# Ring buffers and w_out moved to multiples of 2 KB in a partition, and one block of output products placed earlier in the tail

## The chip, the core and the metric

The kernel runs on one core of a Trainium2 chip. A core has a TensorE (PE, with its weight loads listed apart as PEld), a VectorE (DVE), a ScalarE (ACT), a GpSimd (POOL) and a SyncE (SP), which here only issues transfers, and sixteen DMA engines that carry them. On-chip memory has 128 partitions; a tile occupies the same bytes in each of them. The metric is the device time of one execution in microseconds (us), less is better.

## What is computed

One decoding step of attention over a cached window, gated by a small MLP. From the reference, cut to what matters:

```python
xn = _layernorm(x)                                   # x: (2, 1, 512)
# attention: 32 query heads, 8 key/value heads of 128, window of the last 4096 positions
q = (xn @ wq) as (2, 32, 1, 128)
p = softmax(q . k[:, :, Sk - W:, :] * 128 ** -0.5)
s = (p . v[:, :, Sk - W:, :]) as (2, 1, 4096) @ wo   # wo: (4096, 512)
# gate
z = _gelu(xn @ w_in)                                 # w_in: (512, 1792)
z1, z2 = z[..., :896], _layernorm(z[..., 896:])
g = _silu((z1 * (w_sp * z2 + b_sp)) @ w_out)         # w_out: (896, 512)
out = x + s * g
```

All arrays are float32. Two batches times eight key/value heads are 16 pairs (batch, head); each needs 2 MB of keys and 2 MB of values, and with wq and wo (8 MB each), w_in and w_out the core reads 89.4 MB once.

## The kernel before

**Memory.** Four pools hold the tiles. "cst" (one buffer for each name) has w_out and the small constants; "ring" has four slots of 32 KB in a partition, tagged "slot"; "sb" has the working tiles, two of each; "ps" the accumulators. Pools lie one behind the other in the order in which they are opened (lines 73 to 76). Before the first pool, 128 bytes of a partition hold constants of the framework, behind an area that it reserves; so "cst" begins at byte 16,512, with w_out as its first tile, and "ring" at 55,680.

**The ring.** w_in takes a slot of it, then wq in two slots, then the 16 pairs, keys in the first half of a slot and values in the second, and at last two slots of wo. All these loads are issued by SyncE in program order (lines 89 to 98, "load" in lines 112 to 118, and lines 496 to 509). A load waits until the work that read its slot before is done: for a pair, that is the second product with the values four pairs earlier. Every load covers all 128 partitions, with one piece of consecutive bytes for each partition: 16 KB for keys or values, 28 KB for w_in, 14 KB for w_out, 32 or 16 KB for wq, and 16, 8, 4 or 2 KB for wo. Such a piece is called a row below.

**The attention loop** (lines 462 to 493) interleaves three pairs by hand: for the current one, DVE transposes the keys in four pieces ("turn"), and TensorE multiplies them with the queries ("shares", "scores"); for the one before, maximum, exponentials, and TensorE's product with the values ("pv"); for the one before that, the collection of its heads. The order on every engine is the program's order.

**The tail** (lines 496 to 568). The heads fall into three sets: heads 0 to 3, 4 and 5, 6 and 7. The first two sets' share of wo is loaded as blocks 0 and 1 (8 parts each, 2 MB) and blocks 2 and 3 (4 parts each, 1 MB); the third set's as blocks 4 to 7 (4, 2, 1 and 1 parts). The transfers go in the order of these numbers. "wo_early(n, a0)" multiplies four parts of block n, from part a0, into the accumulator "part", one part for each of the four groups of 32 rows of it; the counter "done" picks the group, and the first four and the last four calls open and close the sums. The products of blocks 2 and 3 stand in a hand-written order among those of block 0 and 1 (lines 540 to 548). Then ACT copies "part" to "parts" (line 550), blocks 4 to 7 are multiplied into "so" as they land, "parts" is added to it by four more products (lines 560 to 564), and DVE applies the gate and adds x.

Of the kernel before, what the change touches and what calls it, by code (L numbers as in the profile page):

```python
# [9 lines left out]
F32 = mybir.dt.float32  # L10
# [4 lines left out]
P = 128  # L15
# [26 lines left out]
def kernel(  # L42
# [27 lines left out]
    DC = D // G  # L70
    SCALE = DH ** -0.5

    cst = ctx.enter_context(tc.tile_pool(name="cst", bufs=1))
    ring = ctx.enter_context(tc.tile_pool(name="ring", bufs=4))
    sb = ctx.enter_context(tc.tile_pool(name="sb", bufs=2))
    ps = ctx.enter_context(tc.tile_pool(name="ps", bufs=1, space=bass.MemoryType.PSUM))

# [435 lines left out]
    def wo_early(n, a0=0):  # L513
        nonlocal done
        t, oT, j = blocks[n]
        for a in range(a0, a0 + 4):
            g = done % G
            pe.matmul(
                part[32 * g : 32 * g + 32, :], oT[:, j + a, :], t[:, a, :], start=(done < G), stop=(done >= EARLY - G)
            )  # L520
            done += 1
# [22 lines left out]
    wo_early(0, 4)  # L544
    wo_early(2)
    wo_early(1, 0)
    wo_early(3)
    wo_early(1, 4)
    parts = sb.tile([P, D], F32, tag="o", name="parts")
    act.activation(parts, part, AF.Copy)  # L550
    so = bank("so", DC)
# [45 lines left out]
```

## Time and profile before

| | us |
|---|---|
| three runs, median | 219.85 |
| the three runs | 219.77, 221.17, 219.85 |
| the profiled execution, device time | 219.7 |
| its span, first to last instruction | 217.6 |
| TensorE busy | 153.0 |
| VectorE busy | 123.4 |
| ScalarE busy | 49.7 |
| mean granted TensorE clock | 0.85 of full |

The profile is of one execution. The span leaves out 2.1 us of the time around the first and last instruction. "Busy" is the time in which an engine had an instruction in work. A row of the forty slices gives, for each slice of 5.44 us, tenths of that slice in which the engine was busy; for the clock, tenths of full speed that were granted to TensorE. In rows of instructions, "out<-in" names the tiles written and read, "x8" counts instructions, and in brackets stand the idle time of the engine just before and what ended it ("issue" is the engine's own sequencing). A product of float32 operands shows as two instructions.

### The profile page before, as it was taken

What the parts mean: (1) busy time and instruction counts of PE and PEld (TensorE: products, weight loads), DVE (VectorE), ACT (ScalarE), POOL (GpSimd) and SP (SyncE); (2) the same over time, 40 slices, a digit from 0 to 9 for tenths busy, and PEclk for the clock granted to TensorE, in tenths of its full rate; (3) what the DMA queues carried; (4) which work ended last, traced back from release to release, by engine and by line L of the source; (5) the groups of instructions that cost most, each with busy time, mean ns of one, the idle gap of its engine ahead of it and who ended that gap; (6) DMA issues with size and microseconds to landing.
All of it is one profiled execution on the core that took longest, in us unless ns stands there. A gap on an engine that the chain in (4) does not pass through costs nothing.

```text
span 217.6 us, 2755 instructions
## 1 busy us (share of the span) xinstructions
PE 153.0 (70%) x1068; PEld 51.8 (24%) x1068; DVE 123.4 (57%) x249; ACT 49.7 (23%) x128; POOL 5.2 (2%) x19
## 2 busy tenths in 40 slices
PE   0179694653898179886788859567995888479593
PEld 0128421300222022221222212112231212124232
DVE  4511212674775577887889494857667494842001
ACT  4110202201213211433223222331142223232000
POOL 8000000000000000000000000000000000000000
PEclk9999589958569755999999978996589589999669
DMA  7999999999999999999999999999999999999990
GB/s 254 425 431 470 392 425 429 428 428 431 425 428 431 428 425 434 425 422 429 428 428 425 428 425 431 429 431 422 428 428 422 428 428 434 434 428 416 416 376 30
DMA packets 6524, 89.57 MB, mean 412 GB/s; under 512 B 734, under 2 KB 750, under 8 KB 1136
## 3 DMA queue, kind: packets, MB, share of 16 engines
q1 hardware_dynamic: 6492, 89.40, 97.0%
q8 instruction: 8, 0.13, 0.2%
q14 instruction: 4, 0.03, 0.0%
q10 hardware_dynamic: 20, 0.01, 0.0%
HBM read 89.40 MB, written 0.00 MB: 411 GB/s over the span
## 4 chain that ended last, share of the span: by engine, by line
DMA 56%; PE 20%; DVE 18%; ACT 3%; issue 1%; SPq 0%; ACTq 0%
DMA kv<-in_A_k_cache_dram 35%; DVE kts L36 14%; DMA wq<-in_A_wq_dram 11%; DMA wo<-in_A_wo_dram 10%; PE acc L36 6%; PE sh L36 4%; PE s L36 3%; PE part L36 3%; PE q_ps L36 2%; DVE m L36 2%; ACT ss L36 1%; PE so L36 1%; ACT p L36 1%; DVE gate L36 1%; DVE pT L36 1%
## 5 line engine op out<-in xcount | busy, mean ns | idle before, releaser
L36 DVE STREAM_TRANSPOSE kts<-kv 128x1024 f32<-128x1024 f32 x64 | 77.2, 1226 | 20.8 <-DMA kv<-in_A_k_cache_dram 20.8
L36 PE MATMUL sh<-kts,qb 128*32 128x512 f32 x256 | 42.5, 740 | 32.8 <-DVE mg L36 24.3
L36 PE MATMUL acc<-kv,pT 128*16 128x512 f32 x256 | 35.0, 669 | 0.0
L36 ACT ACTIVATE o<-acc,wd 128x128 f32<-128x128 f32 x64 | 18.2, 367 | 58.6 <-PE acc L36 50.6
L36 PE MATMUL s<-ss,sums 128*128 128x512 f32 x32 | 21.8, 768 | 6.2 <-ACT ss L36 6.2
L36 ACT ACTIVATE p<-s,nb 128x512 f32<-128x512 f32 x16 | 11.0, 688 | 45.9 <-DVE nb L36 45.9
L36 DVE STREAM_TRANSPOSE pT<-p 128x512 f32<-128x512 f32 x16 | 11.4, 712 | 14.7 <-ACT p L36 14.7
L36 PEld LDWEIGHTS sh<-kts,qb 128*32 128x32 f32 x256 | 6.7, 121 | 51.8 <-issue 37.1
L36 PEld LDWEIGHTS acc<-kv,pT 128*16 128x16 f32 x256 | 6.8, 115 | 26.9 <-issue 19.3
L36 ACT ACTIVATE ss<-sh 128x512 f32<-128x512 f32 x16 | 9.6, 597 | 15.1 <-PE sh L36 13.8
L36 PE MATMUL q_ps<-wq,xnT 128*32 128x512 f32 x64 | 9.3, 704 | 5.1 <-DMA wq<-in_A_wq_dram 5.0
L36 DVE TENSOR_REDUCE m<-s 128x1 f32<-128x512 f32 x16 | 10.5, 657 | 1.4 <-PE s L36 1.4
L36 PEld LDWEIGHTS mo<-l,heads 128*128 128x128 f32 x32 | 5.6, 219 | 17.2 <-ACT p L36 17.2
L36 PE MATMUL part<-wo,oT 128*32 128x512 f32 x48 | 7.9, 792 | 2.3 <-DMA wo<-in_A_wo_dram 2.3
L36 PEld LDWEIGHTS mo<-mg,joint 128*128 128x128 f32 x32 | 5.6, 219 | 16.2 <-issue 15.4
L36 PE MATMUL col<-o,selw 128*32 128x128 f32 x128 | 7.5, 310 | 1.6 <-ACT o L36 1.4
L36 PE MATMUL z<-win,xnT 128*32 128x448 f32 x32 | 4.9, 776 | 4.2 <-DMA win<-in_B_w_in_dram 4.2
L36 PEld LDWEIGHTS s<-ss,sums 128*128 128x128 f32 x32 | 5.6, 219 | 9.2 <-ACT ss L36 6.7
L36 PE MATMUL mo<-l,heads 128*128 128x1 f32 x32 | 6.9, 285 | 0.4
L36 PE MATMUL mo<-mg,joint 128*128 128x8 f32 x32 | 7.1, 293 | 0.0
L36 PE MATMUL zT_ps<-rowm,z 128*128 128x2 f32 x28 | 6.6, 370 | 0.0
L36 DVE TENSOR_TENSOR res<-so,gate 128x128 f32<-128x128 f32 x1 | 0.3, 291 | 11.1 <-PE so L36 11.1
(107 smaller groups left out, 82.9 us busy)
## 6 DMA issues: line engine op xcount, KB each, us to landing
kv<-in_A_k_cache_dram SPq DMA_DIRECT2D x16, 2048.0 KB, 18.9
kv<-in_A_v_cache_dram SPq DMA_DIRECT2D x16, 2048.0 KB, 22.2
wq<-in_A_wq_dram SPq DMA_DIRECT2D x1, 4096.0 KB, 24.4
wq<-in_A_wq_dram SPq DMA_DIRECT2D x2, 2048.0 KB, 30.0
wo<-in_A_wo_dram SPq DMA_DIRECT2D x2, 2048.0 KB
win<-in_B_w_in_dram SPq DMA_DIRECT2D x1, 3584.0 KB
wo<-in_A_wo_dram SPq DMA_DIRECT2D x3, 1024.0 KB, 25.7
wout<-in_B_w_out_dram SPq DMA_DIRECT2D x1, 1792.0 KB, 15.2
```

The lines of the kernel that those rows point to most:

```text
L36: return self.tc.keep_in_program_order(call(*args, **kwargs))
```

## The change

Two edits. The ring's pool is opened ahead of "cst", behind a new pool with one tile "fit" of 480 floats (1,920 bytes in a partition), which nothing writes or reads. The ring thus begins at 16,512 + 1,920 = 18,432, nine times 2,048; its four slots take 131,072 bytes, and w_out, the first tile of "cst", begins at 149,504, 73 times 2,048. The other tiles of "cst" and all of "sb" move as well. In the tail, "wo_early(1, 4)", the second half of block 1, stands ahead of "wo_early(3)" where it stood behind it.

```diff
     SCALE = DH ** -0.5
 
+    fit = ctx.enter_context(tc.tile_pool(name="fit", bufs=1))
+    fit.tile([P, 480], F32, tag="fit", name="fit")
+    ring = ctx.enter_context(tc.tile_pool(name="ring", bufs=4))
     cst = ctx.enter_context(tc.tile_pool(name="cst", bufs=1))
-    ring = ctx.enter_context(tc.tile_pool(name="ring", bufs=4))
     sb = ctx.enter_context(tc.tile_pool(name="sb", bufs=2))
     ps = ctx.enter_context(tc.tile_pool(name="ps", bufs=1, space=bass.MemoryType.PSUM))
...
     wo_early(0, 4)
     wo_early(2)
     wo_early(1, 0)
+    wo_early(1, 4)
     wo_early(3)
-    wo_early(1, 4)
     parts = sb.tile([P, D], F32, tag="o", name="parts")
     act.activation(parts, part, AF.Copy)
```

## The prediction

> **What bounds the kernel now.** I read the page first: the busy shares, the forty slices, the packets and the chain.
>
> ```profile
> span 217.6 us, 2755 instructions
> PE 153.0 (70%) x1068; PEld 51.8 (24%) x1068; DVE 123.4 (57%) x249; ACT 49.7 (23%) x128; POOL 5.2 (2%) x19
> PEclk9999589958569755999999978996589589999669
> DMA  7999999999999999999999999999999999999990
> GB/s 254 425 431 470 392 425 429 428 428 431 425 428 431 428 425 434 425 422 429 428 428 425 428 425 431 429 431 422 428 428 422 428 428 434 434 428 416 416 376 30
> DMA packets 6524, 89.57 MB, mean 412 GB/s; under 512 B 734, under 2 KB 750, under 8 KB 1136
> q1 hardware_dynamic: 6492, 89.40, 97.0%
> DMA 56%; PE 20%; DVE 18%; ACT 3%; issue 1%; SPq 0%; ACTq 0%
> ```
>
> No compute engine is near full: PE is busy for 70% of the span, DVE for 57%. The transfers are: SyncE's queue takes 97.0% of what sixteen DMA engines could give, and every slice but the first and the last reads 9. The rate is flat: from the sixth slice to the thirty-sixth it lies between 422 and 434 GB/s. 89.40 MB at 428 GB/s is 208.9 us of the 217.6, so what else happens in the middle is covered. The chain says the same with 56% for DMA; its PE and DVE pieces are the times at which a buffer was handed back for a transfer that then stood in the queue anyway. Two rows of the DMA issues show how deep that queue is:
>
> ```profile
> kv<-in_A_k_cache_dram SPq DMA_DIRECT2D x16, 2048.0 KB, 18.9
> kv<-in_A_v_cache_dram SPq DMA_DIRECT2D x16, 2048.0 KB, 22.2
> ```
>
> One of these transfers is 2.10 MB, 4.9 us at 428 GB/s, and takes 18.9 or 22.2 us from issue to landing: about four are queued ahead. A slot given back a few us sooner or later doesn't change when the last byte comes.
>
> Then I asked whether the rate depends on what the engines do, by stretches of 24 to 30 us in the middle:
>
> ```profile
> 36.00:60.00 24.00, 14.50 (x113) 4.56 (x113) 14.44 (x20) 3.44 (x7) 0.00 (x0) 0.72 1.01 427
> 60.00:90.00 30.00, 22.63 (x132) 6.37 (x136) 20.59 (x35) 6.51 (x20) 0.00 (x0) 0.71 1.01 430
> 90.00:120.00 30.00, 23.75 (x176) 6.81 (x168) 25.05 (x44) 9.92 (x28) 0.00 (x0) 1.00 1.01 426
> 120.00:150.00 30.00, 20.71 (x148) 6.45 (x147) 20.88 (x35) 7.54 (x21) 0.00 (x0) 0.92 1.01 427
> 150.00:180.00 30.00, 25.21 (x146) 6.83 (x146) 20.54 (x37) 7.60 (x22) 0.00 (x0) 0.74 1.01 428
> ```
>
> The columns are the stretch, its length, busy us of PE, weight loads, DVE, ACT and POOL, then clock, DMA share and GB/s. PE goes from 14.5 of 24 to 25.2 of 30 us, DVE from 14.4 to 25.1, the clock from 0.71 to 1.00; the rate stays at 426 to 430 with a DMA share of 1.01. Nothing but the DMA engines sets the pace here.
>
> Last the tail, by TensorE's timeline and windows cut where the clock changes:
>
> ```profile
> 202.67 1.26 PE L36 MATMUL part<-wo,oT 128*32 128x512 f32 x8
> 206.20 5.62 PE L36 MATMUL part<-wo,oT 128*32 128x512 f32 x32 [2.27 <-DMA wo<-in_A_wo_dram]
> 211.63 1.06 PE L36 MATMUL so<-wo,oT 128*32 128x128 f32 x32
> 212.59 0.43 PE L36 MATMUL so<-parts,rowm 128*32 128x128 f32 x8
> 212.83 1.21 PE L36 MATMUL so<-wo,oT 128*32 128x128 f32 x32
> ```
>
> ```profile
> 199.90:203.40 3.50, 2.63 (x32) 1.28 (x24) 0.48 (x2) 0.88 (x4) 0.00 (x0) 1.00 0.96 405
> 203.40:206.80 3.40, 1.13 (x8) 0.23 (x8) 0.00 (x0) 0.00 (x0) 0.00 (x0) 0.50 1.00 417
> 206.80:210.20 3.40, 3.40 (x20) 0.90 (x16) 0.00 (x0) 0.00 (x0) 0.00 (x0) 0.50 1.02 416
> 210.20:214.10 3.90, 3.84 (x88) 2.16 (x80) 0.00 (x0) 0.60 (x1) 0.00 (x0) 1.00 0.51 196
> ```
>
> TensorE has nothing to do for 2.27 us until block 2 of wo has landed, works without a gap from 206.20 to 214.04, and does the first 4 us of it at half clock (0.50 until 210.2). So after 206.2 it is TensorE that ends the kernel, closely followed by the last transfers: the DMA share falls to 0.51 from 210.2 on.
>
> **The change part by part.** *The layout.* In the allocated program w_out begins at byte 16,512 of a partition and the ring at 55,680: both 128 past a multiple of 256 (55,680 is 27 × 2,048 + 384). The 1,920 bytes of "fit" put the ring at 18,432 = 9 × 2,048; its four slots are 131,072 bytes, so w_out follows at 149,504 = 73 × 2,048. The working tiles of "sb" move up by 1,920. No instruction, wait or transfer is added, removed or moved: "fit" is never written. So the only term can be the time of one access at its new place.
>
> For engine accesses I take nothing. The cover is the stream: a quicker or slower transpose or matmul of the attention only moves hand-backs that are some four transfers early. That holds until DVE, the chain's second worker, is late: it is busy 25.05 of 30 us in the densest stretch, and so would have to become 30 / 25.05, or 20%, slower before it set the pace.
>
> For the transfers there is one term: rate. The trace has no transfer that starts at another alignment, so I bound it by slices. The best inside the plateau read 434 GB/s, the worst 422. All 89.40 MB at 434 take 206.0 us, 2.9 less than at 428; at 422 they take 211.8, 2.9 more. 6524 packets less 734 under 512 B are 5,790 rows, 362 for each engine, so 2.9 us is 8 ns a row. I take zero: the nearest row is the plateau itself, the same through five stretches, and no row of this trace ties a part of those 8 ns to where a row lands.
>
> [...]
>
> *The order in the tail.* Line 548's four products (second half of block 1) now stand ahead of line 547's (block 3). No count changes: the 32 instructions from 206.20 are eight passes over the four column groups either way, two for each call of wo_early. The weight loads show whether block 3 was ever awaited:
>
> ```profile
> 206.17 0.23 PEld L36 LDWEIGHTS part<-wo,oT 128*32 128x32 f32 x8 [3.34 <-issue]
> 207.02 0.23 PEld L36 LDWEIGHTS part<-wo,oT 128*32 128x32 f32 x4 [0.63 <-issue]
> 207.88 0.23 PEld L36 LDWEIGHTS part<-wo,oT 128*32 128x32 f32 x4 [0.63 <-issue]
> 208.73 0.22 PEld L36 LDWEIGHTS part<-wo,oT 128*32 128x32 f32 x4 [0.63 <-DMA wo<-in_A_wo_dram]
> 209.58 0.23 PEld L36 LDWEIGHTS part<-wo,oT 128*32 128x32 f32 x4 [0.63 <-issue]
> 210.34 0.14 PEld L36 LDWEIGHTS part<-wo,oT 128*32 128x32 f32 x4 [0.53 <-issue]
> 210.77 0.13 PEld L36 LDWEIGHTS part<-wo,oT 128*32 128x32 f32 x4 [0.29 <-issue]
> ...
> 213.61 0.16 PEld L36 LDWEIGHTS so<-wo,oT 128*32 128x32 f32 x8 [0.21 <-DMA wo<-in_A_wo_dram]
> ```
>
> One row goes ahead of each pass. At half clock they stand 0.85 us apart, the one marked with block 3's transfer (208.73) included, so the wait cost nothing; at full clock 0.43 (210.34 to 210.77). Behind the swap it is asked for two passes later, 1.7 us at this clock. Nothing is queued behind it on PE that could have gone before, and ACT's copy of "part" still waits for the eighth pass at 211.8. The price is zero. Were the clock full from 206.2 on, block 3 would be asked for three passes of 0.43 us after 206.17, at 207.5, before it is known to be there, and the old order could stall, the new one hardly; but the end would then wait for the last block (asked for at 213.61, with 0.21 of waiting), and no more than about 0.5 us could be won.
>
> Sum: 0 for the engines, 0 for the rate, 0 for the order. The profiled execution took 219.7 us, its span of 217.6 and 2.1 around it; the median of the three runs is 219.85, 0.15 above. I keep 219.7.
>
> **The rivals.** *The rows get cheaper at the new start.* [...] At the full 2.9 us it is 216.8. For it: a stream at 97.0% where only cost per byte can change. Against it: a plateau so flat looks like a plain ceiling.
>
> *Writes and reads collide at the new places.* Rows of 2 KB read by TensorE and rows written by the DMA engines would then begin at the same offsets, and the stream falls to its worst plateau slice, 422 GB/s: 219.7 + 2.9 = 222.6. Since TensorE already waits for the transfers, every us lost is seen; below 423.5 GB/s it costs over 1%. Against it: the rate didn't react to engine load in any of the five stretches.
>
> *The clock falls otherwise in the tail.* Two more passes at half clock cost 0.84 us, with all that follows at half clock too (the products from 211.63 to 214.04) about 3; full clock from 206.2 wins 0.2 to 0.5. That gives 219.3 to 222.7. [...]
>
> *The change does nothing at all* is my forecast.
>
> **How the numbers follow.** The forecast (219.2 to 220.2) gets 0.52, cheaper rows 0.30 (216.8 to 219.2), collisions 0.08 (220.5 to 222.6), the clock 0.10. About 1%, 2.2 us, is what a measurement of this kernel can tell from no change. Faster by more than that (under 217.65) needs a rate above 432.6 GB/s, or 1.7 us with a kind clock: 0.13 of the 0.30. Slower by more (over 222.05): 0.05 of the collisions and 0.02 of the clock, 0.07. The rest, 0.80, lies within. From 217.6 to 220.9 leaves out 0.12 below and 0.08 above.
>
> **What would show it.** The plateau: 428 GB/s again means the rows cost the same; 431 to 434 means they got cheaper; 422 or less a collision. Block 2's landing, by the start of the 32 products, near 206.2 means no gain from the stream. The weight load marked with block 3's transfer should stand two steps later, at unchanged steps, and the products from block 2 to the end should take 7.8 us if the clock returns four us into them. I am wrong if the plateau moves by 4 GB/s or more, or if the tail changes without the clock or the landing having changed.

## Result, and the profile after

| | before | changed |
|---|---|---|
| median, us | 219.76 (10 runs, 219.65 to 221.17) | 218.33 (10 runs, 218.12 to 219.69) |
| ratio | | 0.9933 (95% interval 0.9912 to 0.9954) |

The kernel became 0.67% faster, 1.43 us: inside the range that was given, and not the "no change" that was its likeliest case. One execution of all those reported below, 225.5 us at a granted clock of 0.65 among the twelve with three pairs off, is left out of that run's ratio. The lines of the changed kernel's page that answer to those shown of before:

```profile
span 217.6 us, 2755 instructions
PEclk9999587665599955999889999699958999558598
DMA  7999899999999999999999999999999999999970
GB/s 254 422 434 482 386 428 429 434 434 428 434 419 431 431 434 431 425 434 429 434 431 434 428 431 428 426 434 434 434 425 434 428 434 425 434 428 425 423 303 2
q1 hardware_dynamic: 6492, 89.40, 96.4%
```

The bytes and packets are the same and the span too, yet the last two slices differ: 303 and 2 GB/s where 376 and 30 stood. The transfers were done sooner and the end didn't follow. This profiled execution, 219.69 us, is the slowest of its ten, so its tail is read apart from its stream. First the stream, in the same five stretches (the last column is GB/s):

```profile
36.00:60.00 24.00, 17.67 (x112) 5.60 (x112) 14.39 (x19) 3.15 (x7) 0.00 (x0) 0.59 1.01 431
60.00:90.00 30.00, 21.67 (x136) 6.24 (x136) 20.79 (x36) 7.40 (x22) 0.00 (x0) 0.83 1.01 430
90.00:120.00 30.00, 24.77 (x176) 7.19 (x172) 25.32 (x44) 9.32 (x27) 0.00 (x0) 0.94 1.01 431
120.00:150.00 30.00, 20.89 (x155) 6.10 (x154) 21.07 (x37) 7.95 (x22) 0.00 (x0) 0.94 1.00 429
150.00:180.00 30.00, 21.89 (x144) 6.21 (x140) 20.50 (x35) 8.34 (x24) 0.00 (x0) 0.89 1.01 431
```

The plateau rose: a mean of 430.4 GB/s, against 427.6 before. For all 89.40 MB that is 207.7 us in place of 209.1, 1.4 less. The packet records of the trace, one for each row, say where it comes from:

```
duration of a row, ns      before                          changed
16 KB (4,608 rows)         611 to 625, mean 615.4          611 for 99.6% of them, mean 612.1
 8 KB   (384 rows)         309 to 327, mean 313.7          309
 4 KB   (128 rows)         159 to 172, mean 164.4          159
 2 KB   (256 rows)         84 (median)                     84
```

A few rows are longer than these ranges and count in the means: 14 of 16 KB before (to 1,273 ns) and 10 after (to 1,158), and two of 4 KB before (378 and 440). The shortest row is the same in both kernels for each of these sizes; what has gone is the scatter above it. For each of the sixteen engines that is 288 × 3.3 + 24 × 4.7 + 8 × 5.4 ns = 1.1 us, most of the 1.4 that the rate gives.

TensorE's tail in this execution:

```profile
200.30 3.62 PE L36 MATMUL acc<-kv,pT 128*16 128x512 f32 x16
203.70 1.93 PE L36 MATMUL part<-wo,oT 128*32 128x512 f32 x8
205.40 0.65 PE L36 MATMUL col<-o,selw 128*32 128x128 f32 x8
206.47 1.07 PE L36 MATMUL oT_ps<-o,perm 128*128 128x16 f32 x8 [0.41 <-DVE o L36]
207.46 4.50 PE L36 MATMUL part<-wo,oT 128*32 128x512 f32 x40
211.78 1.06 PE L36 MATMUL so<-wo,oT 128*32 128x128 f32 x32
```

The last pair's product with the values comes late and at half clock (a granted clock of 0.50 from 200.30 to 203.92; 3.62 us), and from 207.46 TensorE works off wo at full clock (1.00 from 206.2 on) without one wait for a transfer. The same kernel, profiled once more (218.34 us in that execution, span 216.2), shows the ordinary case:

```profile
199.94 1.03 PE L36 MATMUL part<-wo,oT 128*32 128x512 f32 x8
...
203.27 1.06 PE L36 MATMUL part<-wo,oT 128*32 128x512 f32 x8
204.91 3.64 PE L36 MATMUL part<-wo,oT 128*32 128x512 f32 x32 [0.57 <-DMA wo<-in_A_wo_dram]
209.81 1.08 PE L36 MATMUL so<-wo,oT 128*32 128x128 f32 x32 [1.26 <-DMA wo<-in_A_wo_dram]
210.68 0.43 PE L36 MATMUL so<-parts,rowm 128*32 128x128 f32 x8
210.97 1.07 PE L36 MATMUL so<-wo,oT 128*32 128x128 f32 x24
212.24 0.43 PE L36 MATMUL so<-wo,oT 128*32 128x128 f32 x8 [0.20 <-DMA wo<-in_A_wo_dram]
```

Here the last pair's product began at 196.63, not 200.30, and took 3.48 us. What differs ahead of it is the clock from 185 to 195 us: 0.53 in the execution of 219.69 us (first line) and 0.94 in this one:

```profile
185.00:195.00 10.00, 8.87 (x38) 2.66 (x42) 5.63 (x12) 1.38 (x3) 0.00 (x0) 0.53 1.00 428
185.00:195.00 10.00, 8.40 (x69) 2.63 (x61) 5.88 (x14) 4.16 (x13) 0.00 (x0) 0.94 1.02 433
```

Block 2 is there at 204.91 where it was at 206.20, 1.3 us sooner, and the last product ends at 212.67 where it ended at 214.04, 1.4 sooner. The whole gain is in the stream, and it arrives at the end.

### The profile page after: what moved, and what is told of

It is laid out like the page before. It is cut to its first block, busy times and chain, and to the rows that moved or that the text cites. A ratio compares the mean times of both kernels' runs of the same rounds, so it can differ in the third digit from the quotient of the medians.

```text
span 217.6 us, 2755 instructions
## 1 busy us (share of the span) xinstructions
PE 156.4 (72%) x1068; PEld 53.3 (24%) x1068; DVE 123.7 (57%) x249; ACT 49.6 (23%) x128; POOL 5.2 (2%) x19
## 3 DMA queue, kind: packets, MB, share of 16 engines
q1 hardware_dynamic: 6492, 89.40, 96.4%
HBM read 89.40 MB, written 0.00 MB: 411 GB/s over the span
## 4 chain that ended last, share of the span: by engine, by line
DMA 52%; PE 28%; DVE 14%; ACT 3%; issue 1%; SPq 0%; ACTq 0%
DMA kv<-in_A_k_cache_dram 41%; DMA wq<-in_A_wq_dram 11%; DVE kts L36 11%; PE acc L36 9%; PE sh L36 6%; PE s L36 5%; PE part L36 3%; PE q_ps L36 2%; ACT ss L36 2%; DVE m L36 2%; PE oT_ps L36 1%; ACT o L36 1%; PE so L36 1%; PE col L36 1%; DVE gate L36 1%
## 5 line engine op out<-in xcount | busy, mean ns | idle before, releaser
L36 PE MATMUL acc<-kv,pT 128*16 128x512 f32 x256 | 36.1, 687 | 0.0
L36 PE MATMUL s<-ss,sums 128*128 128x512 f32 x32 | 22.7, 797 | 6.4 <-ACT ss L36 6.4
L36 PE MATMUL q_ps<-wq,xnT 128*32 128x512 f32 x64 | 10.8, 810 | 5.3 <-DMA wq<-in_A_wq_dram 5.3
L36 PEld LDWEIGHTS zT_ps<-rowm,z 128*128 128x128 f32 x28 | 6.5, 325 | 0.0
L36 PE MATMUL part<-wo,oT 128*32 128x512 f32 x48 | 6.4, 672 | 0.0
```

The lines of the kernel that those rows point to most:

```text
L36: return self.tc.keep_in_program_order(call(*args, **kwargs))
```

## The experiments

Times are medians; ratios are to the kernel before, run on the same chip.

**Which of the two edits.** The layout without the order:

```diff
     wo_early(1, 0)
-    wo_early(1, 4)
     wo_early(3)
+    wo_early(1, 4)
```

> The new layout with the old order in the tail. Theory A (rows written from a multiple of 256 B are not held up: in the changed kernel's packet records every 16 KB row takes 611 ns, where before they took 611 to 622, 615.4 in the mean; 4.4 ns by 288 such rows for each engine are about 1.3 us): nearly the whole gain stays, 218.2 to 218.7 us, plateau 430 to 431 GB/s. Theory B (the order in the tail brings the gain): 219.7. Mixed: in between.

Measured: 218.7 us, ratio 0.9937 (0.9916 to 0.9959), 16 KB rows at 611 ns with a mean of 612.1. The order without the layout is the second hunk of the change alone:

> The old layout with the new order in the tail. Theory A: as before, 219.5 to 219.9 us, plateau 427 to 428 GB/s, rows of 16 KB still scattered from 611 to 622 ns. Theory B: about 218.3.

Measured: 220.07 us, ratio 0.9999 (0.9981 to 1.0018), rows scattered with a mean of 615.5. Four stretches of each show it; first the layout alone:

```profile
60.00:90.00 30.00, 21.61 (x140) 6.12 (x138) 21.41 (x37) 7.74 (x22) 0.00 (x0) 0.83 1.01 431
90.00:120.00 30.00, 24.09 (x174) 6.71 (x172) 24.92 (x41) 8.68 (x25) 0.00 (x0) 0.94 1.01 430
120.00:150.00 30.00, 21.89 (x142) 6.10 (x146) 20.49 (x37) 7.72 (x22) 0.00 (x0) 0.89 1.01 431
150.00:180.00 30.00, 22.79 (x143) 6.48 (x138) 20.09 (x34) 8.10 (x23) 0.00 (x0) 0.82 1.01 430
```

and the order alone:

```profile
60.00:90.00 30.00, 22.24 (x121) 6.11 (x120) 20.45 (x34) 6.59 (x20) 0.00 (x0) 0.76 1.01 429
90.00:120.00 30.00, 23.75 (x182) 6.93 (x182) 24.85 (x46) 9.92 (x28) 0.00 (x0) 1.00 1.00 426
120.00:150.00 30.00, 20.78 (x151) 6.49 (x145) 21.00 (x36) 7.69 (x22) 0.00 (x0) 0.93 1.01 428
150.00:180.00 30.00, 25.36 (x147) 6.86 (x146) 20.81 (x36) 7.54 (x21) 0.00 (x0) 0.73 1.01 428
```

430 to 431 here, 426 to 429 there: the layout has the whole gain, the order none.

**Which start, and whose.** With the new layout and the old order, all tiles were moved on by 256 bytes (544 floats, shown), 128 (512) or 64 (496):

```diff
-    fit.tile([P, 480], F32, tag="fit", name="fit")
+    fit.tile([P, 544], F32, tag="fit", name="fit")
```

> New layout, old order, all tiles moved by a further 256 bytes: ring and w_out begin at a multiple of 256 that is none of 512 or 2,048. If a multiple of 256 is what counts, the same time as with the layout alone (within 0.2 us) and flat rows of 611 ns. If it takes 512 or 2,048, some or all of the gain is gone: 219 to 219.8.

> New layout, old order, all tiles moved by a further 128 bytes, so that ring and w_out begin 128 past a multiple of 2,048. Theory A: the gain is gone, 219.5 to 219.9 us, rows of 16 KB scattered up to 622 ns. If it is the order of the pools and not the start of the rows that helps, the time stays near 218.4.

> New layout, old order, all tiles moved by 64 bytes: ring and w_out 64 past a multiple of 256. If any start off a multiple of 256 is held up alike, 219.6 to 220.1 us and 615 ns for a 16 KB row; if the hold-up goes with the number of bytes in the part block, somewhere between half and one and a half times the loss; if 64 bytes is already a fitting start, 218.4 and flat rows.

Measured: by 256 bytes, 218.45 us (0.9933, 0.991 to 0.9957), block 2's products from 205.08 us (204.98 with the layout alone). By 128, 220.0 us (1.0, 0.9981 to 1.002), mean row 615.5 ns. By 64, 220.02 us (0.9997, 0.9978 to 1.0015), mean row 615.7. So in these runs a multiple of 256 is enough, and 64 past one is as bad as 128; 2,048 isn't needed.

Then the ring was moved against everything else. Ring off by 128, the rest in place:

```diff
-    fit.tile([P, 480], F32, tag="fit", name="fit")
+    fit.tile([P, 512], F32, tag="fit", name="fit")
     ring = ctx.enter_context(tc.tile_pool(name="ring", bufs=4))
+    gap = ctx.enter_context(tc.tile_pool(name="gap", bufs=1))
+    gap.tile([P, 480], F32, tag="gap", name="gap")
```

> New layout, old order, with the ring alone 128 bytes further on; w_out, the constants and the working tiles of sb begin at the same remainders of 2,048 as in the changed kernel. Theory A (it is where the transfers' rows land that counts): the gain is gone, 219.6 to 220.1 us, rows of 16 KB scattered from 611 to 622 ns, 615 in the mean. Theory C (the gain comes from where the engines' working tiles lie): it stays, 218.3 to 218.7 us.

Measured: 219.96 us (1.0001, 0.9992 to 1.0011), mean row 615.3 ns. And the mirror, the ring in place and a gap of 32 floats behind it:

> New layout, old order, the mirror of the run with the ring moved: the ring at its multiple of 2,048, w_out and all constants and working tiles 128 bytes further on. Theory A: 218.3 to 218.8 us and flat rows of 611 ns; w_out is one transfer of forty-five and cannot show. Theory C: 219.6 to 220.1.

Measured: 218.57 us (0.9937, 0.9919 to 0.9954), 430 to 431 GB/s in the four stretches from 60 to 180 us, where the ring off by 128 has 427 to 428. Of the two, the place where the ring's transfers land counts; 128 bytes more or less for the engines' working tiles does not.

**Engines against transfers, or transfers among themselves.** In the kernel before:

```diff
         cur.v = load(cur.n, 1)
+        if 4 <= cur.n < 12:
+            continue
         do(turn, cur, 0)
```

> The kernel before, with the attention's computation left out for pairs 4 to 11 (their keys and values are still loaded; the sums of heads that are missing are set to zero), so that for some 75 us only the transfers run. Theory A1 (off-start rows are held up by engines reading the memory at the same time): in that stretch the 16 KB rows are flat at 611 ns, and 431 GB/s or more is read there. Theory A2 (they are held up by one another, whatever the engines do): the rows stay scattered, 614 to 616 ns in the mean, at 427 to 428 GB/s.

The stretches in which no engine does anything, in the same columns:

```profile
90.00:105.00 15.00, 0.00 (x0) 0.00 (x0) 0.00 (x0) 0.00 (x0) 0.00 (x0) 0.50 1.01 428
105.00:120.00 15.00, 0.00 (x0) 0.00 (x0) 0.00 (x0) 0.00 (x0) 0.00 (x0) 0.50 1.01 428
120.00:135.00 15.00, 0.00 (x0) 0.00 (x0) 0.00 (x0) 0.00 (x0) 0.00 (x0) 0.50 1.01 429
135.00:150.00 15.00, 0.00 (x0) 0.00 (x0) 0.00 (x0) 0.00 (x0) 0.00 (x0) 0.50 1.01 428
```

The rate is that of before, 428, and of the rows in this stretch 74 to 95% in every 4 us are above 611 ns. The engines have no part in it; theory A2 stands, and what holds a row up lies among the transfers. (One execution, 220.54 us; its time is not used.)

**Does a row pay for its own start?** In the changed kernel, with slots longer by 256 bytes, the values alone were put 128 bytes off:

```diff
-            slots[n] = slot(f"kv{n}", 2, NT, DH)
+            slots[n] = slot(f"kv{n}", 2 * NT * DH + 64)
...
+        at = i * (NT * DH + 32)
+        t = slots[n][:, at : at + NT * DH].rearrange("p (j d) -> p j d", d=DH)
```

> The changed kernel with slots 256 bytes longer, so that all starts are multiples of 256, except that the values of each pair begin 128 bytes past one: of the rows, the 16 x 128 of the values are off, all others fit. If a row pays for its own start, about half of the 1.4 us is lost (219.0 to 219.2), and in the packet records stretches of flat and scattered rows alternate every 4.9 us. If off-start rows hold up whatever is under way beside them, or if a few of them spoil the stream as many do, more than half is lost and the rows of the keys scatter too.

Measured: 218.69 us (0.9937, 0.9909 to 0.9965), against 218.48 of the changed kernel in the same session; 4.2% of the 16 KB rows above 611 ns. Neither theory foresaw this: half of the rows are off and next to nothing is lost. The one spot with a visible share is at the end, where the values of pairs 14 and 15 follow each other with no keys between. That led to the last experiment, which puts three pairs of every four off (the edit is against the run just told):

```diff
-        at = i * (NT * DH + 32)
+        at = i * NT * DH + (32 if n % 4 else 0)
```

> The changed kernel with slots 256 bytes longer, keys and values of every fourth pair (0, 4, 8, 12) at multiples of 256, those of the three pairs between 128 bytes past one: six transfers off, about 29 us, then two that fit, about 10 us. The run with the values alone off lost 0.1 to 0.2 us of 1.4, so a row doesn't pay for its own start alone. Theory R (hold-ups build up while off-start rows follow one another, as they did from 30 to 45 us in the runs with all rows off, and rows that fit clear them): in the packet records the share of held-up rows rises within each 29 us and falls after it, and 218.9 to 219.6 us. Theory S (some fitting rows anywhere keep the stream flat): 218.4 to 218.7 and under 5% of the rows held up. Theory P (an off-start row is held up by others under way at the same time that are off): scatter throughout the three pairs, and 219.5 to 219.8.

Measured: 218.97 us (0.9946, 0.9928 to 0.9964). The packet records, taken in the order in which the transfers were issued (K9 is the keys of pair 9; those in brackets fit), with the share of rows above 611 ns:

```
all off (before)   K4 0.79   V4 0.87   K5 0.87  V5 0.73  K6 0.73  K7 0.70  V6 0.84   K8 0.67   V7 0.84  K9 0.80   V8 0.80   K10 0.80  V9 0.73
three pairs off   [K4 0.09] [V4 0.00]  K5 0.00  V5 0.16  K6 0.76  K7 0.56  V6 0.86  [K8 0.09]  V7 0.16  K9 0.82  [V8 0.09]  K10 0.10  V9 0.69
```

The first off-start transfer behind one that fits is nearly free (K5, V7, K10: 0.00 to 0.16), the second or third is not (K6, K9, V9: 0.69 to 0.82), and the next one that fits is nearly free at once, which also ends the run. That is theory R: not the row's own start is paid for, but a run of off-start transfers. The longer slots are not what kept the values' run flat, since these slots have the same length. In the run with the values alone off, keys that fit stand between, and no run forms until V14 and V15 (V15: 0.30). How long a run takes to go bad isn't fixed by this. Behind K8 and V8 it takes one transfer, behind V4 two. But in the first stretch, from K1 to V3, the shares are 0.00, 0.07, 0.08, 0.13, 0.29 and 0.80, though two fitting transfers (K0, V0) went just before; and in the run with all tiles at 128 no row is held up from 6 to 30 us, and 56 to 92% of the 16 KB rows are in every 4 us from 36 us on.

**The tail.** Both halves of block 1 ahead of block 2, in the changed kernel:

```diff
     wo_early(0, 4)
-    wo_early(2)
     wo_early(1, 0)
     wo_early(1, 4)
+    wo_early(2)
     wo_early(3)
```

> The changed kernel with both halves of block 1 multiplied before block 2, in the order in which the transfers land. If the tail is bound by the last transfer, as the profiles with TensorE at full clock there show (it waits for each block), the time stays within 0.2 us of the changed kernel; where the clock is half in the tail, some 1 us is won, so that the scatter upwards (219.7 in one of ten runs) gets less.

> The changed kernel itself, for comparison on the same chip with the two others and, by its ratio to the kernel before, with the layout alone (0.9937): if the order in the tail is worth nothing, 0.993 to 0.994.

Measured: 218.61 us (0.9921, 0.989 to 0.9952), and 218.48 us (0.9912, 0.9879 to 0.9945) for the changed kernel. The tail of the first, by TensorE's timeline:

```profile
201.49 2.78 PE L36 MATMUL part<-wo,oT 128*32 128x512 f32 x24
204.81 1.06 PE L36 MATMUL part<-wo,oT 128*32 128x512 f32 x8 [0.54 <-DMA wo<-in_A_wo_dram]
207.18 1.06 PE L36 MATMUL part<-wo,oT 128*32 128x512 f32 x8 [1.30 <-DMA wo<-in_A_wo_dram]
209.73 1.08 PE L36 MATMUL so<-wo,oT 128*32 128x128 f32 x32 [1.48 <-DMA wo<-in_A_wo_dram]
```

More is done early, and the waits for blocks 3 and 4 only grow (1.30 and 1.48 us). Eight products into "part" take 1.06 us here, against 1.93 at a clock of 0.50 in the execution of 219.69 us (203.70): at this pace the tail waits for the landings in each of the three orders that were run. Block 3 shows the same: the first weight load of its products waits in the old order (first line, the layout alone) and in the new one (second line, the changed kernel), where the steps before it leave 0.27 us:

```profile
207.31 0.16 PEld L36 LDWEIGHTS part<-wo,oT 128*32 128x32 f32 x8 [1.32 <-DMA wo<-in_A_wo_dram]
207.26 0.37 PEld L36 LDWEIGHTS part<-wo,oT 128*32 128x32 f32 x8 [0.48 <-DMA wo<-in_A_wo_dram]
```

TensorE's products then stand still for 0.41 us before block 3 and 0.62 before block 4 in the old order, and for 1.26 before block 4 alone in the new one; the last product ends at 212.72 and 212.67. Whether the scatter upwards gets less, nine runs (218.2 to 219.26) against eight (218.24 to 219.83) don't settle.

Two tails of the old row starts say what TensorE's pace is worth there. With the order alone, the 32 products from block 2 on take 5.63 us, as long as in the kernel before (5.62 us, clock 0.50 until 210.2), and TensorE stands still for nothing afterwards:

```profile
206.61 5.63 PE L36 MATMUL part<-wo,oT 128*32 128x512 f32 x32 [2.34 <-DMA wo<-in_A_wo_dram]
212.06 1.06 PE L36 MATMUL so<-wo,oT 128*32 128x128 f32 x32
213.01 0.43 PE L36 MATMUL so<-parts,rowm 128*32 128x128 f32 x8
213.26 1.18 PE L36 MATMUL so<-wo,oT 128*32 128x128 f32 x32
```

With all tiles at 128 they take 3.84 us, twice 1.92, and TensorE waits three times after block 2:

```profile
206.63 1.92 PE L36 MATMUL part<-wo,oT 128*32 128x512 f32 x16 [0.86 <-DMA wo<-in_A_wo_dram]
209.01 1.92 PE L36 MATMUL part<-wo,oT 128*32 128x512 f32 x16 [0.46 <-DMA wo<-in_A_wo_dram]
211.61 1.08 PE L36 MATMUL so<-wo,oT 128*32 128x128 f32 x32 [0.68 <-DMA wo<-in_A_wo_dram]
...
214.02 0.42 PE L36 MATMUL so<-wo,oT 128*32 128x128 f32 x8 [0.21 <-DMA wo<-in_A_wo_dram]
```

Block 2 starts at 206.6 and the last product ends at 214.44 in both.

## Why the prediction was right or wrong

- **The transfers set the pace.** Right, and stronger than argued: with eight pairs' computation gone the stream's rate is the same (428 to 429 GB/s, against 427.6).
- **Nothing for the engine accesses.** Right: moving the working tiles alone by 128 bytes changes nothing (0.9937 with them off, as with the layout alone).
- **"I take zero" for the rate.** This is the step that failed. The bounds of 2.9 us either way held, and the value was 1.4 on the lower side; the time lies in the range because that had to cover the cheaper rows as well. The reason given was that the plateau stood the same through five stretches of different engine load. That shows the engines have no part, and it is taken as if it showed a ceiling. A plateau can as well be a constant loss, and nothing in it tells the two apart; the spread of the rows' durations does, 611 to 625 ns for rows of one size on engines that never pause. It lies in the packet records of the same trace. The sign for being wrong, 4 GB/s, was too coarse as well, for 1.4 us is 2.8 GB/s; and ten runs of each kernel tell 0.67% from no change (0.9912 to 0.9954), where the prediction took 1% as the least.
- **The rival of cheaper rows.** Its direction was right, and its range, 216.8 to 219.2, holds the 218.33. The "1.7 us with a kind clock" of its chances is a term that no run shows; the runs showed 1.4 us, 1.1 of it in the durations of the rows. No price that every off-start row pays was seen either: the shortest row is 611 ns for 16 KB and 84 ns for 2 KB with either start, and with half of the rows off (the values) 0.2 of the 1.4 us were lost, not half. The boundary that counts here is 256 bytes: a further 256 bytes keeps the whole gain (218.45 us), and 64 or 128 loses it (220.02 and 220.0). Why it is 256, no run shows.
- **Nothing for the order.** Right (0.9999). The reason, that block 3 is never awaited, holds in the tails at half clock (0.50 until 210.2 in the kernel before). In the two executions compared above (sixteen products in 1.92 us, 32 in 3.64) it is awaited in both orders, less in the new one (0.48 us before its weight load, against 1.32), as the prediction's own aside foresaw; but block 4's products start no sooner (209.81 against 209.85), and the last product ends 0.05 us apart, not the 0.5 that the aside allowed.
- **TensorE ends the kernel after block 2.** Only half right. The two tails last shown start alike (206.61 and 206.63) and end alike (214.44), one without a pause at 5.63 us for the 32 products and one with pauses at 3.84: the slower pace from block 2 on used up slack and cost nothing there. In the changed kernel's ordinary execution they take 3.64 us and the whole gain arrives; what a slower pace would leave of it, no execution shows.
- **The clock.** Its scatter exists (219.69 among ten runs), but in the execution shown the cost arose ahead of the tail: at a clock of 0.53 from 185 to 195 us the last pair's product with the values began 3.7 us later than in the execution of 218.34 us. That this product ran at half clock (0.50) is not the reason, since it took 3.62 us in the run with the values off too, and that execution 218.61 us. This rests on single executions.
- **Collisions.** Refuted: the rate rose, from 427.6 to 430.4 GB/s.

## What to carry to other kernels

Where transfers fill the whole time, let every buffer that they land in begin at a multiple of 256 bytes in a partition, which was worth 1.4 us here against starts 64 or 128 bytes past one; small constants in front of a ring, here 128 bytes, are enough to break that, and a filler tile mends it. A flat plateau shows what the rate doesn't depend on and never that it is the ceiling: look at how the durations of equal packets spread. Scattered ones have something to gain, here 3.3 of 615 ns; packets that all take the shortest time may still each pay a price that such a view can't show.

## What the runs showed of the hardware

- With the ring 128 bytes past a multiple of 256, 71% of the 16 KB rows take longer than the shortest of 611 ns, nearly all of these by 1 to 14 ns; the mean is 615.4 ns, against 612.1 at a multiple of 256, and the stream runs at 427.6 GB/s against 430.4. With every engine idle it is the same (428 to 429). With all tiles moved by 64 bytes the mean row is 615.7 ns.
- It needs off-start transfers in a row: one fitting transfer of 2 MB ends it (share of held-up rows 0.86 in V6, 0.09 in K8 behind it), and a stream with every second transfer off ran at nearly full rate (4.2% of its rows above 611 ns, against 71% with all off). Whether the sixteen DMA engines get in each other's way or each is held up behind its own rows wasn't tested, and why no row was held up from 6 to 30 us with all tiles at 128 stays open.
